# A hash-masked attention block with two gated layers on one core: 1/z of seven head pairs spread over the partitions by a store and two repeating loads in place of transposes

## The chip, the cores and the metric

The kernel runs on one core of a Trainium2 chip. The metric is the device time of one execution in microseconds (us). The core has five engines that run side by side, each through its own queue in order: TensorE (PE, with its weight loads PEld), VectorE (DVE), ScalarE (ACT), GpSimd (POOL) and SyncE (SP), which here only issues DMAs. DMAs issued from SP and from ScalarE's queue share 16 DMA engines.

## What is computed

An attention in which a query sees only the keys of its own hash bucket, then two feed-forward blocks on its output. Shapes: q, k, v are (2, 8, 768, 64), the model width is 512.

```python
q_bits = (np.einsum('bhsd,dk->bhsk', q, proj) > 0).astype(np.int64)
k_bits = (np.einsum('bhsd,dk->bhsk', k, proj) > 0).astype(np.int64)
...
mask = q_bucket[:, :, :, None] == k_bucket[:, :, None, :]
scores = scale * np.matmul(q, k.transpose(0, 1, 3, 2))
scores = np.where(mask, scores, -1000000000.0)
scores = scores - np.max(scores, axis=-1, keepdims=True)
attn = np.exp(scores)
attn = attn / (np.sum(attn, axis=-1, keepdims=True) + 1e-09)
return np.matmul(attn, v).astype(np.float32)
...
gated = u * v_s
return (gated @ w_out).astype(np.float32)
...
ch = np.maximum(xn @ w_ch1, 0.0) @ w_ch2
return (x + ch).astype(np.float32)
```

The change concerns one line of this: the division of the attention by its row sum z.

## The kernel before, in words

Nothing is issued where it is written. Every call goes to a planner (class Plan, lines 170 to 508), which groups calls into jobs, gives each a cost, places them by a list schedule with due times, and then issues them engine by engine in that order (line 502 issues everything, so all rows of the profile have that line). A changed job can therefore move its neighbours on every engine.

The program has three parts. The first holds the attention of both batches, and from its second half on the first feed-forward block of batch 0; the second and third parts hold what is left of the feed-forward blocks. The attention runs over 96 tiles (two batches b, eight heads h, six query tiles of 128); `attn_step(i)` (line 922) writes out one step. For a tile it does: `scores` (line 831), four matmuls of the 128 queries against the 768 keys into the PSUM tile sc; `masked_max` (line 843), which takes sc to SBUF as x and the row maximum nb on VectorE; `exps` (line 862), the exponential on ScalarE, whose row sums go to z_sum; `transposes` (line 868), six TensorE transposes pt of x, copied to e by ScalarE and VectorE. After the six tiles of a head, `weighted` (line 885) multiplies e with v: po, whose result, transposed (features on the partitions, queries along the row), is copied to xT. Two heads form a pair (b, r), and share the 128 partitions of xT[b][:, r]: head 2r has partitions 0 to 63, the other head 64 to 127.

This output still has to be divided by z. z lies with queries on the partitions, xT with queries along the row, so 1/z has to be turned and repeated over 64 partitions. Before the change, `summed` (line 902, one tile behind `weighted`) adds 1e-9 and takes the reciprocal zr, 128 x 12. `normalized` (line 909, three tiles behind) spreads zr on GpSimd to zw, 128 x 384 twice, transposes it on TensorE in six pieces of 128x128 into two PSUM banks pz, and VectorE multiplies xT by each bank. Later `x_split` (line 1052) cuts xT into two parts (act_x) for the feed-forward block.

The loads for the scores go through SP. For a pair, q and k are loaded and split in two parts by GpSimd and VectorE; `passes_of` (line 755) then copies, for each head, the pieces of ks (three of 64x768 and two small ones from the mask tile m, 12 rows) and, for each half of the queries, those of qs. v is loaded as vv. These DMAs stand in one order on SP with the stores of the feed-forward block; a DMA whose source isn't ready holds all behind it. PSUM has four banks with the tag b, shared by pt, po, pm, pz and the first block's results, and two double banks for sc.

The planner costs a DMA of SP by the time to issue it and a landing time by kind (lines 186, 187, 239 to 246), and a transpose like any other of its kind (line 249).

## Time and profile before

| | us |
|---|---|
| median of 3 runs | 646.39 (645.65 to 646.8) |
| the profiled execution | 645.79 |
| its span, first to last instruction | 643.6 |
| TensorE busy | 634.8 (99%) |
| VectorE busy | 500.4 (78%) |
| ScalarE busy | 327.7 (51%) |
| GpSimd busy | 189.6 (29%) |

The granted clock of TensorE is 0.999 over the span. The span leaves out the start and the end of an execution, which is why the time is 2.2 us longer. A share of busy time is a mean over the whole program; the attention stage lies between about 20 and 300 us. In the chain of waits a step is as long as it held up the next one, so its steps can be shorter than an instruction's own record. SP's rows show the time it takes to issue a DMA, not the time of the transfer.

### The profile page before, as it was taken

Reading aid. Unit: us, or ns where it says so; the run is one execution under the profiler, and the core shown is the slowest. Engines: PE = TensorE matmul, PEld = TensorE weight load, DVE = VectorE, ACT = ScalarE, POOL = GpSimd, SP = SyncE. Lnnn points to the kernel's source line nnn. Section 1 sums busy time; section 2 is a strip of 40 time slices with the busy share of each in tenths; the row PEclk is TensorE's granted clock in tenths of the full one; section 3 lists DMA queues with packets and bytes.
Section 4 is the critical chain, followed back from the end, with each engine's and each line's share of the span. In section 5 each row is a group of like instructions: output and inputs, shape, how many; then the busy total and the mean of one; then the engine's idle time right before and its main releaser. Section 6 shows DMA issues by size and latency. Waiting matters only on the chain.

```text
span 643.6 us, 10095 instructions
## 1 busy us (share of the span) xinstructions
PE 634.8 (99%) x3506; PEld 520.3 (81%) x3506; DVE 500.4 (78%) x998; ACT 327.7 (51%) x650; POOL 189.6 (29%) x186
## 2 busy tenths in 40 slices
PE   7999999999999999999999999999999999999997
PEld 5777767777787777877888888899999899898896
DVE  6789878797888686886799544699998887969555
ACT  7888877885565655643555323554323333333110
POOL 2142433244554633131343200122122324142200
PEclk9999999999999999999999999999999999999999
DMA  6776676667767877774653240421262626382623
GB/s 153 195 206 155 181 181 154 183 145 240 204 181 243 235 195 212 228 264 176 231 167 145 73 148 17 147 86 46 99 231 114 234 92 223 105 279 74 218 88 143
DMA packets 64738, 107.68 MB, mean 167 GB/s; under 512 B 7008, under 2 KB 33328, under 8 KB 64432
## 3 DMA queue, kind: packets, MB, share of 16 engines
q1 hardware_dynamic: 43232, 67.58, 36.0%
q10 hardware_dynamic: 21456, 39.46, 18.5%
q8 instruction: 28, 0.46, 0.3%
q14 instruction: 22, 0.18, 0.1%
HBM read 63.31 MB, written 24.90 MB: 137 GB/s over the span
## 4 chain that ended last, share of the span: by engine, by line
PE 94%; DMA 2%; DVE 2%; issue 1%; SPq 0%; POOL 0%; ACTq 0%; DVEq 0%; POOLq 0%
PE acc L502 20%; PE p L502 14%; PE pv L502 10%; PE sc L502 10%; PE pt L502 10%; PE po L502 9%; PE pg L502 7%; PE pc L502 5%; PE py L502 5%; DMA qs<-q 2%; PE pm L502 1%; PE pz L502 1%; PE ptr_g L502 1%; PE px_c L502 1%; DMA pj<-in_proj 1%
## 5 line engine op out<-in xcount | busy, mean ns | idle before, releaser
L502 PE MATMUL acc<-w,ch 128*128 128x512 f32 x576 | 142.9, 393 | 0.0
L502 PEld LDWEIGHTS acc<-w,ch 128*128 128x128 f32 x576 | 107.3, 188 | 18.9
L502 ACT ACTIVATE x<-x,nb 128x768 f32<-128x768 f32 x96 | 89.7, 936 | 31.3 <-DVE x L502 26.4
L502 DVE TENSOR_SCALAR_CACHE_REDUCE x<-sc 128x768 f32<-128x768 f32 x96 | 90.9, 951 | 6.8 <-PE sc L502 3.7
L502 PE MATMUL sc<-ks,qs 128*128 128x512 f32 (+3 forms) x384 | 93.8, 363 | 1.9 <-DVE x L502 1.2
L502 POOL TENSOR_TENSOR f64c_w<-f_w,f64c_w 128x512 f32<-128x512 f32 x32 | 44.1, 1380 | 152.9 <-issue 81.8
L502 PE MATMUL pt<-ident,x 128*128 128x128 f32 x576 | 81.3, 274 | 0.3 <-DVE xT L502 0.3
L502 PEld LDWEIGHTS pt<-ident,x 128*128 128x128 f32 x576 | 66.5, 140 | 14.9 <-issue 2.4
L502 PEld LDWEIGHTS sc<-ks,qs 128*128 128x128 f32 (+1 forms) x384 | 62.9, 190 | 13.9 <-issue 2.2
L502 PE MATMUL po<-e,vv 128*64 128x384 f32 x384 | 65.5, 490 | 0.0
L502 ACT ACTIVATE ch<-u 128x384 fp32r<-128x384 f32 x48 | 25.2, 525 | 79.1 <-DVE u L502 67.0
L502 ACT ACTIVATE e<-pt 128x384 f32<-128x384 f32 x120 | 55.0, 485 | 18.6 <-PE pt L502 18.1
L502 DVE TENSOR_TENSOR u<-p,u 128x384 f32<-128x384 f32 x84 | 45.4, 552 | 20.5 <-PE p L502 20.0
L502 PEld LDWEIGHTS po<-e,vv 128*64 128x64 f32 x384 | 26.1, 137 | 31.2 <-issue 29.8
L502 PE MATMUL p<-t,w 128*128 128x384 f32 x252 | 50.0, 337 | 0.0
L502 PE MATMUL p<-xh,w 128*128 128x384 f32 x252 | 48.8, 338 | 0.0
L502 DVE COPY e<-pt 128x384 f32<-128x384 f32 x72 | 39.7, 553 | 9.6 <-PE pt L502 9.0
L502 PEld LDWEIGHTS p<-t,w 128*128 128x128 f32 x252 | 44.9, 188 | 2.3
L502 PEld LDWEIGHTS p<-xh,w 128*128 128x128 f32 x252 | 44.6, 188 | 2.2 <-DVE u L502 0.3
L502 POOL TENSOR_TENSOR w<-f64c_w,w 128x512 fp32r<-128x512 f32 (+1 forms) x28 | 35.2, 1259 | 37.8 <-ACT w L502 15.0
L502 DVE TENSOR_SCALAR f64c_w<-f64c_w 128x512 f32<-128x512 f32 x64 | 30.8, 480 | 18.5 <-ACT f64c_w L502 15.8
L502 PE MATMUL pg<-vn,w_sp 128*128 128x512 f32 x180 | 43.6, 396 | 0.0
(155 smaller groups left out, 1018.5 us busy)
## 6 DMA issues: line engine op xcount, KB each, us to landing
f_w<-in_w ACTq DMA_DIRECT2D x32, 512.0 KB
ots<-y_dram SPq DMA_DIRECT2D x12, 768.0 KB
ks<-k SPq DMA_DIRECT2D x45, 192.0 KB
y_dram<-ots SPq DMA_DIRECT2D x30, 256.0 KB
qs<-q SPq DMA_DIRECT2D x30, 192.0 KB
wst_sp<-in_w_spT SPq DMA_DIRECT2D x12, 384.0 KB
vv<-in_v SPq DMA_DIRECT2D x16, 192.0 KB
qs<-q SPq DMA_DIRECT2D x30, 96.0 KB
```

The lines of the kernel that those rows point to most:

```text
L502: res = getattr(getattr(nc, engine[j.engine]), op)(*map(live, args), **{k: live(x) for k, x in kw.items()})
```

## The change

`summed` now keeps zr by head, and for seven of the eight pairs does more: one TensorE transpose of the 128 x 12 tile zr into a PSUM bank, a VectorE copy of the 12 x 128 result to zt, a store of zt to a DRAM tile zd, and two loads from zd, each of which repeats one head's row of 768 values over 64 partitions, into zb (128 x 768). `normalized` for such a pair stands eight tiles behind `weighted` in place of three, and is one VectorE multiply of xT by zb, both in SBUF. The last pair (1, 3) keeps the way of before, three tiles behind, with its broadcast in four pieces. There is one buffer each for zt and zb (and the last pair's zw).

```diff
--- before.py
+++ after.py
@@ -901,21 +901,40 @@
 
     def summed(b, r):
 
-        zr = ap.tile([P, NQT, 2], F32, tag="zr", name=f"zr_{b}_{r}")
-        nc.vector.tensor_scalar(zr, z_sum[b][:, :, 2 * r : 2 * r + 2], 1e-9, None, op0=ALU.add)
+        zr = ap.tile([P, 2, NQT], F32, tag="zr", name=f"zr_{b}_{r}")
+        for h in range(2):
+            nc.vector.tensor_scalar(zr[:, h], z_sum[b][:, :, 2 * r + h], 1e-9, None, op0=ALU.add)
         nc.vector.reciprocal(zr, zr)
         pairs[b, r]["zr"] = zr
+        if (b, r) == (B - 1, H // 2 - 1):
+            return
+        rows = 2 * NQT
+        pz = ps_b.tile([P, GW], F32, tag="b", name=f"pz_{b}_{r}")
+        nc.tensor.transpose(pz[:rows, :P], zr.rearrange("p h a -> p (h a)"), ident)
+        zt = ap.tile([rows, P], F32, tag="zt", name=f"zt_{b}_{r}", bufs=1)
+        nc.vector.tensor_copy(zt, pz[:rows, :P])
+        zd = dram.tile([2, 1, S], F32, tag=f"zd_{b}_{r}", name=f"zd_{b}_{r}")
+        nc.sync.dma_start(out=zd.rearrange("h o (a q) -> (h o a) q", a=NQT), in_=zt)
+        zb = ap.tile([P, S], F32, tag="zw", name=f"zb_{b}_{r}", bufs=1)
+        for h in range(2):
+            nc.sync.dma_start(out=zb[h * D : (h + 1) * D], in_=zd[h].to_broadcast([D, S]))
+        pairs[b, r]["zb"] = zb
 
     def normalized(b, r):
 
+        if "zb" in pairs[b, r]:
+            nc.vector.tensor_tensor(xT[b][:, r], pairs[b, r]["zb"], xT[b][:, r], op=ALU.mult)
+            return
         zr = pairs[b, r]["zr"]
+        both = ap.tile([P, S], F32, tag="zw", name=f"zw_{b}_{r}", bufs=1)
         for c in range(2):
-            zw = ap.tile([P, 6, D], F32, tag="zw", name=f"zw_{b}_{r}_{c}", bufs=2)
-            zc = zr[:, c * 3 : c * 3 + 3, :].rearrange("p a (h o) -> p (a h) o", o=1)
-            nc.gpsimd.tensor_scalar(zw, zc.to_broadcast([P, 6, D]), 1.0, 0.0, op0=ALU.mult, op1=ALU.add)
+            zw = both[:, c * KC : (c + 1) * KC].rearrange("p (a h d) -> p a h d", a=3, h=2)
+            for h in range(2):
+                zc = zr[:, h, c * 3 : c * 3 + 3].rearrange("p (a o) -> p a o", o=1)
+                nc.gpsimd.tensor_scalar(zw[:, :, h], zc.to_broadcast([P, 3, D]), 1.0, 0.0, op0=ALU.mult, op1=ALU.add)
             pz = ps_b.tile([P, 3, P], F32, tag="b", name=f"pz_{b}_{r}_{c}")
             for i in range(3):
-                nc.tensor.transpose(pz[:, i, :], zw[:, 2 * i : 2 * i + 2].rearrange("p h d -> p (h d)"), ident)
+                nc.tensor.transpose(pz[:, i, :], zw[:, i].rearrange("p h d -> p (h d)"), ident)
             xs = xT[b][:, r, c * KC : (c + 1) * KC]
             nc.vector.tensor_tensor(xs, pz.rearrange("p a n -> p (a n)"), xs, op=ALU.mult)
 
@@ -934,8 +953,10 @@
             exps(*order[i + 1])
         if 0 <= i - PO < NT and order[i - PO][2:] == (NG - 1, GRP - 1):
             weighted(*order[i - PO][:2])
-        for late, e in ((1, summed), (3, normalized)):
+        for late, e in ((1, summed), (3, normalized), (8, normalized)):
             n = i - PO - late
+            if late > 1 and (late == 8) == (n == NT - 1):
+                continue
             if 0 <= n < NT and order[n][1] % 2 == 1 and order[n][2:] == (NG - 1, GRP - 1):
                 e(order[n][0], order[n][1] // 2)
         n = i + 1 + QA
```

How this moves instructions shows at three places. In the rows, sc is a score tile by head, half and tile, pt the transpose of a tile's exponentials, ks and qs the operands of the scores, pz the transposed 1/z. The first place is TensorE around pair (0, 1), first before, then with the change:

```order
L502 MATMUL pt_4_1_0_0_976<-ident,x_4_1_0_917 128x128 x3
L502 MATMUL pt_4_1_0_1_983<-ident,x_4_1_0_917 128x128 x3
L502 MATMUL sc_4_1_2_992<-ks_4_0_690,qs_4_384_823 128x512 x2
L502 MATMUL sc_4_1_2_992<-ks_4_0_690,qs_4_384_823 128x256 x2
L502 MATMUL pz_1_0_1001<-ident,zw_1_0_947 128x128 x3
L502 MATMUL pz_1_1_1011<-ident,zw_1_1_952 128x128 x3
L502 MATMUL sc_5_0_0_1016<-ks_5_0_857,qs_5_0_912 128x512 x2
L502 MATMUL sc_5_0_0_1016<-ks_5_0_857,qs_5_0_912 128x256 x2
```

```order
L502 MATMUL sc_4_1_2_958<-ks_4_0_675,qs_4_384_807 128x512 x2
L502 MATMUL sc_4_1_2_958<-ks_4_0_675,qs_4_384_807 128x256 x2
L502 MATMUL pt_4_0_2_1_966<-ident,x_4_0_2_883 128x128 x3
L502 MATMUL pz_1_974<-ident,zr_1_853 12x128
L502 MATMUL pt_4_1_0_0_979<-ident,x_4_1_0_907 128x128 x3
L502 MATMUL pt_4_1_0_1_985<-ident,x_4_1_0_907 128x128 x3
L502 MATMUL sc_5_0_0_995<-ks_5_0_843,qs_5_0_902 128x512 x2
L502 MATMUL sc_5_0_0_995<-ks_5_0_843,qs_5_0_902 128x256 x2
```

Two groups of three 128x128 transposes have become one transpose of 12x128, which stands in the run of the pt transposes, earlier in the order.

The second place is SP around pair (0, 3), where the operands of head 2 of batch 1 are copied; before, then with the change:

```order
L502 DMA ks_2_0_1731<-k_1_1_1654 64x768 x2
L502 DMA qs_2_0_1774<-q_1_1_1656 64x2x384
L502 DMA qs_2_0_1774<-m_1_1777 12x384
L502 DMA ks_2_0_1731<-m_1_1777 12x384
L502 DMA ks_2_0_1731<-k_1_1_1654 64x768
L502 DMA qs_2_0_1774<-q_1_1_1656 64x384
L502 DMA ks_2_0_1731<-m_1_1777 12x384
```

```order
L502 DMA ks_2_0_1704<-k_1_1_1640 64x768 x2
L502 DMA zd_3_1725<-zt_3_1707 12x128
L502 DMA qs_2_0_1762<-q_1_1_1636 64x2x384
L502 DMA zb_3_1775<-zd_3_1725 64x768 x2
L502 DMA ks_2_0_1704<-m_1_1760 12x384
L502 DMA qs_2_0_1762<-m_1_1760 12x384
L502 DMA qs_2_0_1762<-q_1_1_1636 64x384
L502 DMA ks_2_0_1704<-k_1_1_1640 64x768
L502 DMA ks_2_0_1704<-m_1_1760 12x384
```

The store of zd and the two loads of zb stand between the first two ks_2 loads and the other DMAs that complete ks_2 and qs_2.

The third place is TensorE where that ks_2 is first read; before, then with the change:

```order
L502 MATMUL sc_1_1_2_1851<-ks_1_0_1547,qs_1_384_1696 128x512 x2
L502 MATMUL sc_1_1_2_1851<-ks_1_0_1547,qs_1_384_1696 128x256 x2
L502 MATMUL pt_1_0_2_1_1857<-ident,x_1_0_2_1788 128x128 x3
L502 MATMUL pt_1_1_0_0_1866<-ident,x_1_1_0_1828 128x128 x3
L502 MATMUL sc_2_0_0_1872<-ks_2_0_1731,qs_2_0_1774 128x512 x2
L502 MATMUL sc_2_0_0_1872<-ks_2_0_1731,qs_2_0_1774 128x256 x2
```

```order
L502 MATMUL sc_1_1_2_1838<-ks_1_0_1535,qs_1_384_1671 128x256 x2
L502 MATMUL pt_1_0_2_1_1844<-ident,x_1_0_2_1770 128x128 x3
L502 MATMUL pt_1_1_0_0_1853<-ident,x_1_1_0_1816 128x128 x3
L502 MATMUL pt_1_1_0_1_1862<-ident,x_1_1_0_1816 128x128 x3
L502 MATMUL sc_2_0_0_1868<-ks_2_0_1704,qs_2_0_1762 128x512 x2
L502 MATMUL sc_2_0_0_1868<-ks_2_0_1704,qs_2_0_1762 128x256 x2
```

The second group of pt_1_1_0 now stands ahead of the first sc_2_0 instead of behind it.

## Rows read from the trace of the kernel before

**Rows 1.** The page's head: span, then busy us (share) x instructions of each engine.
```profile
span 643.6 us, 10095 instructions
PE 634.8 (99%) x3506; PEld 520.3 (81%) x3506; DVE 500.4 (78%) x998; ACT 327.7 (51%) x650; POOL 189.6 (29%) x186
```

**Rows 2.** Waits of TensorE, whole span: us in total, times, longest us.
```profile
PE sc L502 <- DVE x L502: 1.2, 2, 0.9
PE sc L502 <- DMA qs<-q: 0.5, 1, 0.5
PE pt L502 <- DVE xT L502: 0.3, 1, 0.3
```

**Rows 3.** Busy us by stretch, 20 to 300 us; last TensorE clock, DMA share, GB/s.
```profile
20.00:60.00 40.00, 39.48 (x269) 27.96 (x268) 34.41 (x72) 33.16 (x72) 14.06 (x15) 1.00 0.71 181
...
100.00:140.00 40.00, 40.00 (x275) 28.49 (x274) 35.20 (x74) 31.07 (x69) 11.07 (x12) 1.00 0.65 162
...
sum 280.00, PE 278.87 PEld 207.88 DVE 227.17 ACT 188.40 POOL 108.82; mean PE 39.84 PEld 29.70 DVE 32.45 ACT 26.91 POOL 15.55
```

**Rows 4.** Chain of waits, 20 to 60 us: start us, length us, what.
```profile
26.91 5.21 DMA qs<-q
...
46.48 0.24 PE sc L502 x2
46.72 0.66 PE pz L502 x6
47.38 0.70 PE sc L502 x4
48.08 0.33 PE pt L502 x3
```

**Rows 5.** Tiles pz and zr: ns min/median/max, first and last start us, shapes.
```profile
L502 PE MATMUL pz<-ident,zw x48: 269/273/330, 46.6 to 302.6; 128*128 128x128 f32 x48
L502 DVE TENSOR_TENSOR xT<-pz,xT x16: 547/552/558, 47.9 to 303.7; 128x384 f32<-128x384 f32 x16
...
L502 POOL TENSOR_SCALAR zw<-zr x16: 510/512/941, 36.3 to 294.6; 128x384 f32<-128x384 f32 x16
L502 DVE TENSOR_SCALAR zr<-z_sum x8: 161/169/1323, 34.1 to 293.6; 128x12 f32<-128x12 f32 x8
```

**Rows 6.** Groups of VectorE, shapes apart: busy us, mean ns of one; idle before.
```profile
L502 DVE COPY e<-pt 128x384 f32<-128x384 f32 x72 | 39.7, 553 | 9.6 <-PE pt L502 9.0
L502 DVE SCALAR_TENSOR_TENSOR q<-q 128x768 fp32r<-128x768 f32 x7 | 9.2, 1320 | 0.0
...
L502 DVE TENSOR_TENSOR w_sp_early<-wst_sp,w_sp_early 128x768 fp32r<-128x768 f32 x2 | 1.8, 924 | 0.0
```

**Rows 7.** SP in order of time, 128 to 136 us: start us, us to issue.
```profile
128.85 1.12 SPq L502 DMA_DIRECT2D ks<-k  x2
...
132.11 0.80 SPq L502 DMA_DIRECT2D qs<-m  x1
132.96 0.76 SPq L502 DMA_DIRECT2D ks<-m  x1
133.83 0.52 SPq L502 DMA_DIRECT2D ks<-k  x1
134.49 0.51 SPq L502 DMA_DIRECT2D qs<-q  x1
135.06 0.78 SPq L502 DMA_DIRECT2D ks<-m  x1
```

**Rows 8.** Waits of SP for stores to DRAM, whole span: total, times, longest us.
```profile
SPq L502 <- DMA y_dram<-ots: 8.6, 4, 3.7
...
SPq L502 <- DMA y_dram<-ot: 1.6, 1, 1.6
```

**Rows 9.** VectorE and TensorE in order of time, 131 to 140 us.
```profile
131.41 0.67 DVE L502 TENSOR_SCALAR m<-pm,above,worth 128x384 fp32r<-128x384 f32 x1
...
139.61 0.96 PE L502 MATMUL sc<-ks,qs 128*128 128x512 f32 x4
```

## The prediction, made before the changed kernel was run

> **What bounds the kernel now.** I read the page's head first, then the waits of TensorE, then the busy times by stretch, then the chain of waits, and last the timeline around the places that the change touches. The head shows TensorE busy for 634.8 of 643.6 us and the next engine, VectorE, for 500.4 [rows 1]. The list of TensorE's waits is nearly empty: the reader should see three short rows, with nothing above 0.9 us at one time [rows 2]. In the attention stage, 20 to 300 us, TensorE is busy 278.87 of 280 us, VectorE 227.17, GpSimd 108.82, and the DMA engines carry a share of 0.71 in the first stretch [rows 3]. So the rest of the kernel runs into a TensorE queue that is always full, and what leaves that queue in this stage comes off the end. The chain of waits says the same in small: sc, pz and pt follow each other with no step between them, and six pz transposes take 0.66 us of it [rows 4]. The one long DMA step of that chain, 5.21 us for a qs load, is also the one place where TensorE waited for a load, 0.5 us [rows 2, 4].
>
> **The change, part by part.** TensorE loses 42 of the 48 pz transposes (seven pairs of six) and gains seven transposes that write 12x128.
> - Removed: seven times 0.66 us [rows 4] = 4.62 us, all of it on the path.
> - Added: seven times one transpose of zr. No row of before has that form. The nearest is a transpose that streams the same 128 columns inside a run, 0.66 / 6 = 0.11 us [rows 4]; the other end is one that overlaps nothing, its whole record of 273 ns [rows 5]. I take 0.11, since the chain has the queue full on both sides: 0.77 us, with 1.91 as the far end.
> - TensorE together: -4.62 + 0.77 = -3.85 us, or -2.71 at the far end.
>
> The record of one transpose is 273 ns, yet six of them take 0.66 us of the chain, so I price by the chain [rows 4, 5]. The Trainium skill, "TensorE: Matmul & The Clock Gate", section "Part 4: PE-mode transpose", gives about 275 ns for a 128x128 transpose in a kernel's context; taken as the price, the sum would be near -9.6 us, an estimate from that page. The record agrees with the page and the spacing does not.
>
> VectorE loses two multiplies from PSUM of 552 ns per pair, keeps the reciprocal, has two small adds (169 ns) in place of one, and gains a copy of 12x128 (between the 169 ns of a small operation [rows 5] and the 553 ns of a 128x384 copy) and one multiply of 128x768 in SBUF (between 924 and 1320 ns) [rows 5, 6]. Per pair that is +0.16 to +0.92 us, and 1 to 6.4 us over seven pairs, beside 280 - 227 = 53 us in which VectorE is idle in this stage [rows 3]. I cost it at nothing; if that cover were gone, 6.4 us would be the price. GpSimd loses 14 broadcasts of 512 ns [rows 5], 7.2 us; nobody waits for them, so nothing is gained. The last pair keeps its six transposes; its broadcast is cut into four pieces instead of two. In before the last broadcast starts at 294.6 and the last transpose of it at 302.6 us [rows 5], so these eight microseconds hide it and it counts as nothing. The PSUM bank of pz is held for a short copy instead of until a multiply, which can only help.
>
> DMA: each pair adds a store of 6 KB and two loads that repeat a 3 KB row over 64 partitions, 2 x 192 KB. Seven pairs are 2.7 MB; at the 181 GB/s that a share of 0.71 carries [rows 3] the full rate is about 255 GB/s, so this is some 11 us of the 280, and the share goes from about 0.71 to 0.75. Bandwidth has room; landing times may not.
>
> SP is the queue to look at, because it issues in order and a load of zb may not go before the store of zd has landed. In six of the seven pairs, other work or an idle stretch of SP lies between store and load, or nothing behind it is urgent. The tight one is pair (0, 3). In the order of the change, its store stands behind two ks_2 loads, with one qs_2 load after it and then both zb loads, ahead of the five DMAs that complete ks_2 and qs_2. In before, the two ks loads end issuing at 128.85 + 1.12 = 129.97 us, and the last ks<-m ends at 135.06 + 0.78 = 135.84 [rows 7]. A small DMA takes 0.8 us to issue and a ks load 0.56, so with the change the store leaves SP at 130.8, and the zb loads leave 1.1 us after it has landed. How long a landing takes has no row of its own: the shortest wait of SP for a store is 1.6 us, the longest 3.7 [rows 8], and the longest DMA step of the chain 5.2 [rows 4]. At 1.6 us SP is free at 133.5; the five DMAs behind take 3.7 us with their gaps, so the last ends at 137.2, 1.4 us later than before. The mask rows m, for which the first of them waits, are ready at 131.41 + 0.67 [rows 9] and no longer decide. TensorE wants ks_2 at 139.61 [rows 9], 3.8 us after 135.84, and the change puts one more group of three transposes (0.33) ahead of it, so 4.1 us. What is left over is 1.4 plus the landing of that last piece minus 4.1: nothing at a landing of 1.6, 1.1 us at 3.8, which is the most it can have been in before, since TensorE did not wait there. I take 0.4.
>
> The multiplies are the other new wait. Where zb lands late, VectorE stands still and the row maxima behind the multiply come late to ScalarE and so to the pt transposes. The place of the multiply is 14 rows of order behind the zt copy in pair (0, 3) and ten behind the next pair's in pair (0, 0). With 40 us for 74 instructions in that stretch [rows 3], and a second instruction behind each row maximum, these are about 10 and 7 us, against two landings and 2 us of issuing, or one landing and 2 us. At 1.6 us a landing nothing waits, at 3.7 pair (0, 3) is about level. I take 0.2 us in all.
>
> Sum: -3.85 + 0.4 + 0.2 = -3.25 us. The profiled execution took 645.79 us, so 642.5. The median of the runs, 646.39, lies 0.6 above it, which gives 643.1 for a median after. The later stages keep their order nearly unchanged and I let them shift as a block.
>
> **The rivals.**
> - *Part of the gain goes into late landings (0.20).* With a store that lands after 3.7 us, SP comes 3.5 us later to the end of ks_2, and TensorE waits 1.0 to 3.2 us at 139 us, say 2.1. Then -3.85 + 2.1 = -1.75: 644.0 for the profiled run, 644.6 as a median, up to 645.7. For it speaks the share of 0.71 and the chain's qs step; against it that SP's waits in before for stores are few.
> - *TensorE was not what paced the stage (0.09).* Its weight loads are busy only 28.49 us of 40 in the third stretch, and VectorE 35.20 [rows 3]. If matmuls were being held by operands while they count as busy, leaving some out would only lengthen other holds. That would give 646.4. The Trainium skill, "Perfetto Trace Analysis", section "Identifying the Most-Contended Engine", says just this, that matmul busy time is a poor measure and weight-load busy time a better one; by it TensorE would have a quarter to spare here. Against it stand the gapless chain and the empty list of waits [rows 2, 4].
> - *Slower: the store and load hold SP and starve ks_2 (0.10).* One mechanism: if both the store of zd and the last piece of ks_2 take a time L to land, the wait at 139 us is (L - 0.2) + L - 4.1. It eats the whole 3.85 us from L = 4.1 on. At L = 5.2, the longest step of the chain, it is 6.1 us: 645.79 - 3.85 + 6.1 = 648.0, a median of 648.6. For it speaks that the zb loads, 384 KB, stand directly ahead of these pieces; against it, that the 5.2 us occurred once.
> - *Each transpose costs its record (0.01).* (42 - 7) x 0.273 = 9.6 us [rows 5], so 636.8. The chain speaks against it. The figure of the Trainium skill, "TensorE: Matmul & The Clock Gate", section "Part 4: PE-mode transpose", would lead to nearly the same time.
>
> **How the numbers follow.** The forecast has the remaining 0.60: 643.1, by itself 641.7 to 644.0, which is the price ends of the transpose (-2.71 to -3.85) with 0 to 0.6 us of waits, and the spread of the runs of before, 0.7 us down. The range runs from 641.6 to 646.6: it takes in the first two rivals and leaves out the slower case, the transposes at full record and some of each tail, less than 2 in 10. A difference of 0.2%, 1.3 us, is about what a measurement of this kernel can tell from no change. Below 645.1 lie the forecast, most of the late-landing case (0.12) and the last rival: 0.73. Between lie the rest of the late-landing case and most of the second rival: 0.16. Above 647.7: 0.11.
>
> **What would show it.** In the profile after: pz with seven transposes of 12x128 and six of 128x128, TensorE's busy time lower by about 4 us, and its list of waits still short. The rows on which the forecast would fall: a wait of PE sc for a DMA on ks near 136 us, SP waiting for zd by more than 4 us, VectorE xT waiting for zb by more than a microsecond in several pairs, or a TensorE busy time that stays at 634 with fewer instructions, which is the second rival.

## The result and the profile after: slower by 4 us

The changed kernel took 649.86 us (median of 5, 648.74 to 650.07), the kernel before beside it 645.81 (644.83 to 646.8). The ratio is 1.0056 with an interval of 1.0042 to 1.007, so it is slower, by about 3.6 to 4 us. The forecast was 643.1 with a range up to 646.6: wrong in sign. The slower rival had a chance of 0.10 and gave 648.6, but by a mechanism that did not occur, as the runs below show.

First the page's head of the kernel after (span; then busy us, share and instructions of each engine), which answers to [rows 1]:

```profile
span 648.0 us, 10076 instructions
...
PE 634.9 (98%) x3471; PEld 517.3 (80%) x3471; DVE 507.6 (78%) x1006; ACT 327.1 (50%) x650; POOL 186.0 (29%) x174
```

TensorE has 35 instructions fewer and is busy for 634.9 us, against 634.8 before. The prediction had named this row as the one that would show its second rival: a busy time that stays when work is taken away. That fits matmuls which are held by something else and count as busy; the row alone doesn't show it, because the span grew as well.

The parts themselves are as priced. Here are the tiles pz, zt and xT after (durations in ns as min/median/max, then the first and last start in us, and the shapes), which answer to [rows 5, 6]:

```profile
L502 PE MATMUL pz<-ident,zr x7: 272/272/275, 42.7 to 258.9; 128*12 128x128 f32 x7
L502 DVE COPY zt<-pz x7: 268/269/275, 44.6 to 259.9; 12x128 f32<-12x128 f32 x7
...
L502 DVE TENSOR_TENSOR xT<-zb,xT x7: 940/958/1080, 80.0 to 282.1; 128x768 f32<-128x768 f32 x7
```

The copy took 269 ns and the large multiply 958, inside the bounds that were given. TensorE's waits (total, times, longest, in us), against [rows 2]:

```profile
PE sc L502 <- DVE x L502: 1.8, 3, 0.7
PE sc L502 <- DVE f64c_u L502: 1.8, 1, 1.8
PE pv L502 <- DVE e L502: 1.5, 1, 1.5
...
PE p L502 <- DVE u L502: 1.4, 2, 0.8
```

No row names ks, and between 125 and 150 us, around the place that I had picked, its list of waits is empty. And the chain of waits looks different. Its shares between 26 and 136 us, the first half of the attention (batch 0), in the kernel before:

```profile
by line: PE sc L502 32.4%; PE pt L502 29.1%; PE po L502 27.5%; DMA qs<-q 4.7%; PE pm L502 2.8%; PE pz L502 2.4%; SPq L502 0.7%; issue 0.5%
```

and in the kernel after, same view and stretch:

```profile
by line: PE sc L502 22.4%; PE po L502 21.0%; PE pt L502 20.0%; DVE x L502 10.5%; ACT x L502 6.0%; ACT e L502 2.7%; issue 2.4%; DVE f64c_v L502 2.2%; PE pm L502 2.1%; DVE e L502 1.8%; POOL f64c_v L502 1.6%; DVE xT L502 1.6%; DVE q L502 0.9%;
```

Before, the chain is TensorE plus one qs load. After, a tenth of it is VectorE's row maximum x, and 6% ScalarE's exponential. These shares are a hint and no more: e1 and e14 below have the change's order in this stretch and no DMAs of the change, and x has 2.3% of the chain in one and 5.4% in the other. The time can be located better by the starts of the po groups, one for each of the 16 heads, which are the same work in every kernel (from the instructions of tile po in the traces; one profiled execution each, us; "last po" is the start of the last group):

| kernel | first po | first po of batch 1 | last po | first half | second half | last po to the end of the span |
|---|---|---|---|---|---|---|
| before | 25.4 | 133.9 | 298.0 | 108.5 | 164.1 | 345.6 |
| after | 24.7 | 136.3 | 300.2 | 111.6 | 163.9 | 347.8 |
| e9, 42 transposes out | 26.2 | 135.8 | 297.8 | 109.6 | 162.0 | 345.7 |
| e12, 14 multiplies out | 26.3 | 133.9 | 298.5 | 107.6 | 164.6 | 345.7 |
| e13, both out | 26.0 | 133.1 | 295.0 | 107.1 | 161.9 | 346.9 |
| e14, no DMAs, later parts as before | 25.5 | 133.4 | 296.0 | 107.9 | 162.6 | 345.9 |
| e15, e16, e17, first half as before | 26.8, 26.3, 26.5 | 134.7, 134.0, 134.1 | | 107.9, 107.7, 107.7 | | |

The change lost 3.1 us in the first half, gained 0.2 in the second instead of the 1.65 that three pairs should bring, and lost 2.2 after the attention. The last row shows how far one execution can be trusted: e15 to e17 have the first half of the kernel before, and it took 0.6 to 0.8 us less there than in the profile of before. So a tenth or two means nothing here, and the loss in the first half is 3 to 4 us.

### The profile page after: what moved, and what is told of

The parts are those of the page before. It is cut to its first block, busy times and chain, and to the rows that moved or that the text cites. A ratio compares the mean times of both kernels' runs of the same rounds, so it can differ in the third digit from the quotient of the medians.

```text
span 648.0 us, 10076 instructions
## 1 busy us (share of the span) xinstructions
PE 634.9 (98%) x3471; PEld 517.3 (80%) x3471; DVE 507.6 (78%) x1006; ACT 327.1 (50%) x650; POOL 186.0 (29%) x174
## 4 chain that ended last, share of the span: by engine, by line
PE 78%; DVE 8%; DMA 4%; ACT 3%; issue 3%; SPq 1%; POOL 1%; ACTq 0%; DVEq 0%; POOLq 0%
PE acc L502 18%; PE p L502 12%; PE pv L502 9%; PE sc L502 8%; PE po L502 7%; PE pt L502 7%; PE pg L502 6%; PE pc L502 5%; PE py L502 4%; DVE x L502 2%; DMA zb<-zd 2%; ACT x L502 2%; DMA qs<-m 1%; SPq L502 1%; DVE f64c_w L502 1%
## 5 line engine op out<-in xcount | busy, mean ns | idle before, releaser
L502 PEld LDWEIGHTS acc<-w,ch 128*128 128x128 f32 x576 | 107.1, 188 | 19.0
L502 PEld LDWEIGHTS pt<-ident,x 128*128 128x128 f32 x576 | 67.1, 142 | 14.3 <-issue 3.2
L502 PEld LDWEIGHTS po<-e,vv 128*64 128x64 f32 x384 | 26.2, 137 | 31.4 <-issue 29.6
L502 POOL TENSOR_TENSOR w<-f64c_w,w 128x512 fp32r<-128x512 f32 (+1 forms) x28 | 36.6, 1309 | 33.3 <-ACT w L502 13.5
L502 DVE TENSOR_SCALAR f64c_w<-f64c_w 128x512 f32<-128x512 f32 x64 | 36.7, 574 | 11.6 <-ACT f64c_w L502 10.2
```

The costliest lines, as they stand in the source:

```text
L502: res = getattr(getattr(nc, engine[j.engine]), op)(*map(live, args), **{k: live(x) for k, x in kw.items()})
```

## Experiments

Each ratio is to the kernel before, run on the same chip beside it, with its 95% interval. Medians of before were 645.7 to 646.1 in all groups of runs. Where I state a difference of two kernels from different groups, it is a difference of their ratios times 646.

### What the DMAs cost, and by what

**e1: the change without its DMAs.** At issue time, the stores and loads are skipped, and the multiply reads xT twice, so that the kernel leaves the 1/z out of seven pairs.

```diff
                 for op, args, kw in j.calls:
+                    if op == "dma_start" and of(kw["out"])[:3] in ("zd_", "zb_"):
+                        continue
+                    if op == "tensor_tensor" and of(args[1]).startswith("zb_"):
+                        args = (args[0], args[2], args[2])
```

> The changed kernel's own order on every engine, but the seven stores of zd and the fourteen loads of zb are not issued, and the seven multiplies read xT twice in place of zb and xT (so the output lacks the division for these pairs). Theory 1, the added DMAs lose the time: the waits of TensorE near 90, 115, 207 and 297 us go, and the time falls by 4 to 7 us, to 643 to 646. Theory 2, the new order of all other instructions loses the time: nothing changes beyond 1 us, 649 to 650. Theory 3, the multiplies hold VectorE: as theory 1 here, and told apart from it by the next kernel.

Measured: 646.83 us, ratio 1.0019 (1.0009 to 1.0029). The DMAs cost about 0.0037 x 646 = 2.4 us here, but without them the change is still not faster.

**e2: the DMAs stay, the multiply does not wait for them.** Only the second of the two edits of e1.

> The same order, with all stores and loads of zd and zb issued, but no multiply waits for them: the seven multiplies read xT twice (the division is missing for these pairs). Theory 1 (the DMAs delay the loads of ks and qs): 649 to 650 as with the change. Theory 3 (VectorE stands still for zb, 5.3 us in four waits): 1 to 4 us less, 646 to 648.5. Theory 2: 649 to 650.

Measured: 648.84 us, ratio 1.0059 (1.004 to 1.0078), the same as the change. So VectorE's wait for zb, which in the trace after is the row below, costs nothing that can be measured; the DMAs do their harm to others.

```profile
DVE xT L502 <- DMA zb<-zd: 5.3, 4, 2.1
```

**e6 and e7: size or order?** In e6 each load of zb brings 2 partitions; in e7 it is whole, but repeats a row of the input, so that it waits for no store. In both the multiply reads xT twice, as in e2.

```diff
+                    if op == "dma_start" and of(kw["out"])[:3] == "zb_":
+                        kw = {"out": kw["out"][:2], "in_": kw["in_"][:2]}                          # e6
+                        kw = {"out": kw["out"], "in_": qT[0, 0, 0:1].to_broadcast([64, 768])}      # e7
```

> The change in its own order, every DMA kept with its waits, but each load of zb brings 2 partitions instead of 64 (6 KB in place of 192 KB); the multiply reads xT twice, so this kernel leaves the 1/z out of seven pairs. Theory A (the bytes of the repeating loads delay the loads of ks, qs and vv): like the kernel without the DMAs, 646.4 to 647.3. Theory B (the store that has to land holds SP, and what stands behind it goes late): like the kernel whose multiply reads xT but which keeps the DMAs, 648.4 to 649.3. In between, both have a part.

> The change in its own order, the stores of zd kept and both loads of zb at full size, but they repeat a row of the input qT, so that they wait for no store; the multiply reads xT twice, so this kernel leaves the 1/z out of seven pairs. Theory A (the bytes): 648.4 to 649.3, as with the DMAs kept whole. Theory B (SP held until the store has landed): 646.4 to 647.3, as without the DMAs.

Measured: e6 646.65 us, ratio 1.001 (1.0002 to 1.0019), as without the DMAs. e7 649.3 us, ratio 1.0048 (1.003 to 1.0066), as with them whole. It is the size of the loads (e6 cuts their bytes and their rows, 64 of 3 KB, together, so these two are not told apart). The wait of SP for the store of zd, on which the sum and the slower rival rested, is not what costs.

How 192 KB can matter is seen at one place. SP between 78 and 92 us in the kernel after (start us, us to issue):

```profile
81.35 0.50 SPq L502 DMA_DIRECT2D zb<-zd  x1
82.31 0.35 SPq L502 DMA_DIRECT2D vv<-in_v  x1
83.91 1.34 SPq L502 DMA_DIRECT2D qs<-q  x2
85.29 0.79 SPq L502 DMA_DIRECT2D qs<-m  x1
```

and TensorE behind it (the bracket is the idle time before):

```profile
88.30 0.48 PE L502 MATMUL sc<-ks,qs 128*128 128x256 f32 x2
90.54 0.71 PE L502 MATMUL sc<-ks,qs 128*128 128x512 f32 x2 [1.77 <-DVE f64c_u L502]
```

This sc is the first reader of the qs loads issued at 83.91 to 86.08. The bracket names a VectorE instruction, but e6, with the same order and 6 KB in place of 192, issued its qs loads at 84.22 and ran through this place without a wait. The semaphore records of the two traces settle it: the three qs loads had landed at 90.03, 90.41 and 90.59 us in the kernel after, and at 88.50 to 88.88 in e6. TensorE's queue was released at 90.41, and this sc began at 90.54. So qs landed late, behind the zb load and the vv load. (The chain shown above follows the same bracket into VectorE's work, so part of VectorE's share of it is this load.) Where the names are plain they say it: TensorE's waits in e7 between 100 and 120 us and in e2 between 88 and 120 have one row each,

```profile
PE sc L510 <- DMA qs<-q: 1.8, 1, 1.8
```

```profile
PE sc L508 <- DMA qs<-q: 1.4, 1, 1.4
```

against two waits of 0.8 us together in e6 from 80 to 120. The wait has a tail. Stretches of four microseconds (the columns are the busy times of PE, PEld, DVE, ACT and POOL, the granted clock, DMA share, GB/s), after:

```profile
82.00:86.00 4.00, 4.00 (x29) 3.50 (x28) 3.37 (x7) 2.25 (x6) 1.74 (x1) 1.00 0.72 230
86.00:90.00 4.00, 2.78 (x20) 2.25 (x18) 4.00 (x13) 4.00 (x11) 0.00 (x0) 1.00 0.97 213
90.00:94.00 4.00, 3.46 (x16) 3.05 (x17) 1.70 (x4) 1.74 (x4) 1.31 (x1) 0.68 0.48 106
94.00:98.00 4.00, 4.00 (x24) 1.93 (x24) 1.30 (x4) 2.99 (x6) 0.12 (x1) 0.89 0.79 248
```

and in e6:

```profile
82.00:86.00 4.00, 4.00 (x28) 3.19 (x24) 3.34 (x8) 1.93 (x5) 1.73 (x1) 1.00 0.54 174
86.00:90.00 4.00, 4.00 (x29) 3.44 (x29) 4.00 (x12) 4.00 (x10) 0.00 (x0) 1.00 0.96 217
90.00:94.00 4.00, 4.00 (x30) 2.45 (x30) 2.18 (x7) 4.00 (x10) 1.30 (x1) 1.00 0.69 148
94.00:98.00 4.00, 4.00 (x30) 2.76 (x27) 3.19 (x7) 1.68 (x4) 2.75 (x3) 1.00 0.71 232
```

After the wait of 1.77 us TensorE was granted a clock of 0.68 and 0.89 for two stretches, where it has 1.00 in e6, and it got through 16 and 24 matmuls instead of 30. The DMA share of 0.71 in the prediction is a mean: here it is 0.97 and 0.96 for four microseconds in the two kernels, and what is already under way at that moment decides.

The starts of po show that such places are the whole of what the DMAs cost in the first half. All these kernels have the change's order of the attention (us):

| kernel | first to fifth po | fifth to sixth | sixth to ninth | ninth to last | TensorE's waits at these places |
|---|---|---|---|---|---|
| e1, no DMAs | 53.4 | 13.2 | 41.5 | 163.1 | 0.7 at 117 |
| e14, no DMAs | 53.5 | 13.0 | 41.4 | 162.6 | 0.6 at 117 |
| e6, short loads | 53.5 | 13.2 | 41.7 | 162.7 | 0.3 at 117 |
| after | 53.4 | 16.5 | 41.6 | 163.9 | 1.8 at 91, 0.7 at 117 |
| e2 | 53.6 | 14.7 | 43.9 | 163.1 | 1.4 at 91, 1.6 at 120 |
| e3 | 53.4 | 13.9 | 44.0 | 164.2 | 0.6 at 90, 1.8 at 115 |
| e7 | 53.4 | 13.4 | 44.4 | 164.9 | 1.8 at 118 |
| e8, loads from GpSimd | 53.8 | 14.3 | 42.1 | 164.8 | 1.1 at 91, 1.5 at 119 |

Seven pairs load zb, but in the first half only two places lose time, both where a qs load is issued soon after a zb load; how the loss is shared between them differs from execution to execution. With each wait of 1.6 to 1.8 us came stretches of 4 us at a granted clock between 0.68 and 0.89 (after, e2 at 120, e3, e7), and the stretch lost 2.4 to 3.3 us against e1; after the waits of 1.1 to 1.5 us of e2 at 91 and of e8 the clock stayed at 1.00 and the loss was about that of the wait or less.

**e8: the DMAs issued by GpSimd** (the later parts as in e3, below).

```diff
+                    who = "gpsimd" if op == "dma_start" and of(kw["out"])[:3] in ("zd_", "zb_") else engine[j.engine]
```

> The change with its later parts in the order of the kernel before (647.9 us when it was run with its DMAs on SP), and the stores of zd and loads of zb issued by GpSimd instead of SP. Theory B (SP's in-order wait): the loads of ks and qs go on time, and the time falls to about 645, under the kernel before. Theory A (bytes on the shared DMA engines): 647 to 649, no better than on SP. Risk in both: GpSimd stands until the store has landed, and what it computes for VectorE goes late.

Measured: 647.97 us, ratio 1.0037 (1.0025 to 1.005), the same as e3 with its DMAs on SP (1.0036). Freeing SP of the wait brings nothing, which agrees with e6 and e7. Here the loads go through a queue of their own and not through SP's, and TensorE still waits for qs loads (1.8 us in two places). So it is not the place in SP's queue by itself that costs, which leaves the 16 DMA engines that the queues share; that GpSimd, standing for the store, took back a gain elsewhere is not ruled out.

### What the new order costs

**e3: the later parts in the order of before.** The kernel's planner first runs over the old form; parts two and three then take their places from that run.

```diff
+    def pin(self):
...
+        for j, k in self.keys():
+            if j.part < 1:
+                continue
...
+            j.start, j.end = self.pins[k][:2]
```

> The change as it is, with the second and third part of the program (everything after the attention) put into the order that these parts have in the kernel before; the first part keeps the changed kernel's order. After 300 us the changed kernel falls back by another 2 to 3 us against before. If that is its later order: 2 to 3 us less, 647 to 648. If it is a consequence of how the attention ended or of the clock: no change, 649 to 650.

Measured: 647.88 us, ratio 1.0036 (1.0023 to 1.0049). The later order alone costs 0.0020 x 646 = 1.3 us (by the medians 2.0), with an interval from about 0.1 to 2.5. The traces put it nearer to 2: from the last po to the end of the span all kernels with the change's later order take 347.7 to 348.8 us (after, e1, e2, e6, e7), and those with the order of before 345.6 to 346.2, apart from e13 (346.9). The chain of waits from 400 to 640 us shows where it lies. Before it is all TensorE, apart from 0.6% of ots_last; after:

```profile
by line: PE acc L502 42.1%; PE p L502 31.4%; PE pc L502 7.9%; issue 2.7%; DMA f64c_w<-kept 2.4%; PE py L502 2.3%; PE pg L502 1.7%; DVE f_w L502 1.6%; DVE ots L502 1.6%; DVE f64c_w L502 1.5%; DVE u L502 1.3%; PE px_c L502 1.1%; DVE ch L502 0
...
482.32 5.76 DMA f64c_w<-kept
```

In e3 it is TensorE's again. The second row is a weight that is read back from DRAM, with VectorE's work around it. I had not looked at these parts of the order at all: the change has no instruction there, but the planner's times moved, and with them much of the order of VectorE and ScalarE behind the attention.

**e14: e3 without the DMAs**, which tells what is left when both costs are gone.

> The change with the later parts in the order of the kernel before (647.9 us with its DMAs), the stores of zd and loads of zb not issued; the multiply reads xT twice, so this kernel leaves the 1/z out of seven pairs. If the bytes (2 to 3 us) and the later order (2 us) add up: 644.5 to 645.5. If they are not independent: 646 or more.

Measured: 644.72 us, ratio 0.9985 (0.9976 to 0.9994). This kernel is faster than before: the work that the change moves, with the new order of the attention, is worth 1.0 us, the DMAs cost (1.0036 - 0.9985) x 646 = 3.3, the later order 1.3, in all 3.6 us slower. These three must add up to 1.0056, since each is a step from one kernel to the next; taken in the other sequence, by e1, the DMAs cost 2.4 and the later order 2.2, which agrees within the intervals. What is left to explain is why 3.85 us were only 1.0.

### Were the transposes on the path?

**e9: before, without the 42 transposes.** No transpose is put in their place, the multiplies read xT twice, and the order is that of before.

```diff
+                    if op == "transpose" and of(args[0]).startswith("pz_") and not of(args[0]).startswith("pz_1_3"):
+                        continue
+                    if op == "tensor_tensor" and of(args[1]).startswith("pz_") and not of(args[1]).startswith("pz_1_3"):
+                        args = (args[0], args[2], args[2])
```

> The kernel before, in its own order, with the 42 pz transposes of the seven pairs left out and nothing put in their place; their multiplies stay where they were and read xT twice, so this kernel leaves the 1/z out of seven pairs. Theory (TensorE's queue paces the attention): 4.6 us less, 641.2, the lost time of TensorE as before. Rival (TensorE is not the pacer, its holds only move): 644 to 646, with TensorE's list of waits or its busy time grown by what was left out.

Measured: 645.35 us, ratio 0.9994 (0.9984 to 1.0003): no difference, where the prediction had 4.62 us. TensorE's busy time is 634.7 with 42 instructions fewer. Its chain from 26 to 136 us, beside that of before shown above:

```profile
by line: PE po L510 29.7%; PE sc L510 24.6%; PE pt L510 24.3%; DMA qs<-q 4.7%; DVE x L510 4.4%; ACT x L510 2.9%; issue 2.1%; PE pm L510 2.1%; DVE xT L510 1.9%; DVE f_u L510 1.0%; DVE e L510 0.9%; ACT e L510 0.7%; ACT f64c_v L510 0.6%; SPq L
```

With the transposes gone, steps of VectorE and ScalarE come up at once. By the table of po starts the second half became 2.1 us shorter (18 transposes by 0.11 are 1.98), and the first half 1.1 us longer although 24 left it. But e9 does not take away the transposes alone: its multiplies, which now read two operands from SBUF, became longer. VectorE between 20 and 300 us, before and in e9 (busy us, mean ns):

```profile
L502 DVE TENSOR_TENSOR xT<-pz,xT 128x384 f32<-128x384 f32 x14 | 7.4, 551 | 0.0
```

```profile
L510 DVE TENSOR_TENSOR xT<-xT 128x384 f32<-128x384 f32 x14 | 11.2, 825 | 0.0
```

Of these 3.8 us, 0.8 lie in the first half, 0.7 of it in one multiply at 73.5 us, and the head in which it stands took 15.3 us against 14.5 to 14.9 in the kernels with the same order there (before, e12, e13, e15 to e17).

**e12 and e13: the multiplies out; and both out.**

```diff
+                    if op == "tensor_tensor" and of(args[1]).startswith("pz_") and not of(args[1]).startswith("pz_1_3"):
+                        continue                                                                   # e12 and e13
+                    if op == "transpose" and of(args[0]).startswith("pz_") and not of(args[0]).startswith("pz_1_3"):
+                        continue                                                                   # e13
```

> The kernel before with the 14 multiplies by 1/z of the seven pairs left out on VectorE (their output is not scaled), the 42 transposes kept. If VectorE's work paces the first half of the attention: 642 to 644 (four pairs of 1.1 us and less). If TensorE paces it, or both are level: within 1 us of the kernel before.

> The kernel before with both the 42 transposes and the 14 multiplies of the seven pairs left out (their output is not scaled). If TensorE and VectorE are level, so that either alone gains little: clearly less than with the transposes or the multiplies left out alone, 641 to 643. If something else paces (ScalarE, the DMAs): 644.5 to 646.

Measured: e12 645.71 us, ratio 0.9998 (0.999 to 1.0007), no difference. e13 643.76, ratio 0.9969 (0.9957 to 0.9981), 2.0 us less. Between e12 and e13 only the 42 transposes differ, so this pair is the cleaner test: the transposes are worth 0.0029 x 646 = 1.9 us (about 0.9 to 2.8) of the 4.62 forecast.

By the starts of po this gain lies in the second half, which took 161.9 us against 164.6 in e12. Two pairs show their price there:

| us | before, e12 (transposes kept) | e9, e13, e17 (left out) |
|---|---|---|
| tenth to eleventh po, pair (1, 0) | 25.1, 25.1 | 24.4, 24.4, 24.4 |
| fourteenth to fifteenth po, pair (1, 2) | 27.8, 27.8 | 27.1, 27.1, 27.1 |

That is 0.7 us per pair, the 0.66 that the chain gave; the place of pair (1, 1) varies more and shows no such step. In the first half 24 transposes are worth about 0.5 us or less: it took 107.1 in e13 against 107.6 in e12, one execution each, and the kernels of the change's order without large loads, with 20 transposes fewer there, took 107.9 to 108.4 (e1, e6, e14), no less than before. What paces the first half stays open. Two loops that are nearly level, TensorE and the way through VectorE's row maximum, ScalarE's exponential and back, would explain e9 and e12; but e13 takes 2.6 us from the one and 4.4 from the other, and half a microsecond is all that comes of it. That e13 took 1.3 us longer behind the attention is not explained either (one profiled execution).

**e17: the change in the second half alone, without its DMAs**, in the order of before.

> The change in the second half alone without its stores and loads; the multiply reads xT twice, so this kernel leaves the 1/z out of three pairs. If TensorE paces the second half: 15 transposes fewer, 1.65 us, so 644.0 to 645.0. If not: 645.5 to 646.5.

Measured: 644.63 us, ratio 0.9982 (0.9971 to 0.9993): 1.2 us less of the 1.65. So in the second half, TensorE does pace. In the change these 1.65 us shrank to 0.2 for two reasons that the po starts show: a wait of 1.5 us near 210 us for e (the row of pv above), which e1 has too and before does not, so it is the new order; and 0.8 us in the last head, which e1, e6 and e14 do not have, so it is the loads.

### The change by hand in the order of before

**e4, e5, e10, e11.** All engines keep the order of before; the change's instructions are put in at chosen places (pz 2 us after the reciprocal, the copy 0.5 us later in e4 and e5 and 5 us later in e10 and e11, the loads 6 or 10 us after pz, the multiply 15 or 19). e5 and e10 are without the DMAs.

```diff
...
+                    (0, "PE", "transpose", f"pz_{nm}", None, 0, pz),
+                    (0, "DVE", "tensor_copy", f"zt_{nm}", None, 0, pz + 0.5),
+                    (0, "SP", "dma_start", f"zd_{nm}", None, 0, pz + 1.0),
+                    (0, "SP", "dma_start", f"zb_{nm}", None, 0, pz + self.LOADS),
...
```

> The change in the order of the kernel before: every instruction that both have keeps its place of before on each engine, and the new ones are put in by hand (per pair the 12x128 transpose 2 us behind the reciprocal, the store 1 us behind it, both loads of zb 6 us behind the transpose, the multiply 15 us behind it or, for pair (0, 3), just ahead of its first reader). Theory 2 (order): the full gain of 3.9 us less some tenths, 642 to 643. Theory 1 (DMAs): the loads still delay ks and qs, 645 to 649.

> The hand-placed kernel (order of the kernel before everywhere, the change's instructions put in by hand), with the stores of zd and the loads of zb not issued; the multiply reads xT twice, so this kernel leaves the 1/z out of seven pairs. Theory (42 - 7 transposes are worth 3.9 us on TensorE's path, and the DMAs and the new orders take them back): about 3.9 us under the kernel before, 641 to 643, TensorE busy about 4 us less than before and its list of waits as short as before's. Rival (TensorE was not the pacer, its holds only move): within 1 us of the kernel before, with TensorE's busy time near 634.

> As the hand-placed kernel without the DMAs (648.1 us), but the copy of zt stands 4.5 us later in VectorE's order, so that VectorE does not stand behind the po group for pz (4.9 us of such waits in that kernel between 20 and 140 us); the multiply reads xT twice, so this kernel leaves the 1/z out of seven pairs. If that hold of VectorE was the loss: 642 to 643.5. If the loss is in the rest (the transposes were no path, or the 128x768 multiply): 646 to 648.

> The change with the order of the kernel before everywhere, the copy of zt 4.5 us later than in the first hand-placed kernel, the DMAs on SP. If the copy's hold was the loss there and the bytes of the loads cost about 2 us: 644 to 645.5, at or a little under the kernel before. If the transposes were no path: 648 to 650.

Measured: e4 649.78 us, ratio 1.0067 (1.0051 to 1.0082); e5 648.07, 1.0036 (1.0024 to 1.0048); e10 649.01, 1.0045 (1.0028 to 1.0061); e11 654.55, 1.0134 (1.0115 to 1.0152). e5 was the first sign that the term of TensorE was wrong: no DMAs, the order of before, 35 transposes fewer, and 2.3 us slower. VectorE's waits in e5 (20 to 140 us) offered a cause of my own making, the copy of zt standing behind a po group for pz:

```profile
DVE zt L571 <- PE pz L571: 4.9, 2, 3.2
```

e10 moved the copy out of that wait and was not faster, which speaks against this cause. It doesn't rule it out: VectorE's waits at zt and xT together were 6.8 us in this stretch of before, 9.5 in e5 and still 8.2 in e10. What makes the hand-placed kernels slower than e9 stays open; they put a second small add, a copy and a longer multiply at new places into an order of VectorE that was laid out without them. The 4.8 us that e11 took more than e4 lie at one place of the second half, which is also that of e15 below: from the twelfth to the thirteenth po it took 31.5 us, against 26.3 in before.

**e15 and e16: the change in the second half alone, with its DMAs**, by hand in the order of before. In e16 the loads of pair (1, 1) stand behind the load of w_spT.

```diff
-    COPY, LOADS, MULT = 2.5, 6.0, 15.0
+    COPY, LOADS, MULT = 2.5, (6.0, 14.0, 6.0), (15.0, 25.0, 15.0)
```

> The change for the pairs (1, 0) to (1, 2) alone, the other five with the transposes, everything in the order of the kernel before. If TensorE paces the second half: 18 - 3 transposes are 1.65 us less, the loads of three pairs give back up to 1, so 644.3 to 645.5, a little under the kernel before. If the loads cost more, or TensorE does not pace there either: 645.8 or more.

> As the kernel with the change in the second half alone (648.7 us), but the two loads of zb of pair (1, 1) are issued behind the load of w_spT and the qs load that stood behind them, and its multiply 10 us later. If the loads' place was the loss: 644.3 to 645.5, under the kernel before. If the loads lose as much at another place: 647 or more.

Measured: e15 648.73 us, ratio 1.0046 (1.0029 to 1.0062). Its chain has the reason (start, length, what):

```profile
202.41 4.28 DMA zd<-zt
...
207.94 0.79 SPq L563
...
209.33 7.61 DMA wst_sp<-in_w_spT
```

and the waits of ScalarE from 196 to 222 us:

```profile
ACT w_sp L563 <- DMA wst_sp<-in_w_spT: 3.8, 1, 3.8
```

384 KB of weights behind 384 KB of zb took 7.61 us; ScalarE stood for them 3.8 us in its order, and the copies and exponentials behind it with it. In the kernel before, this load was issued at 208.1 us and ScalarE began with it at 212.9, so it took at most 4.8 us; here it was issued at 209.3, and ScalarE began at 217.0. With the loads moved behind it, e16 took 647.38 us (645.6 to 648.98), ratio 1.0018 (1.0005 to 1.003): 1.8 us better than e15, still not under the kernel before, with a wait of 1.7 us for ScalarE's xT left in TensorE's list. No version with the repeating loads beat the kernel before.

## Why the prediction was wrong, step by step

- **"What leaves that queue in this stage comes off the end"** is the step that failed first. The rows were read nearly rightly: a gapless chain and almost no waits [rows 2, 4]. (Over the whole span TensorE has two more waits, of 1.4 and 1.3 us, which [rows 2] leaves out; both lie before 20 us.) They show that TensorE ends last at each step, not by how much. A chain of waits names the one that comes last, by however little; e9 took 24 transposes out of the first half and got nothing, and e13 against e12 got 0.5 us. Of the 3.85 us for TensorE, 1.0 came (e14), and by the table it came in the second half (162.6 us against 164.1). The rival "TensorE was not what paced the stage", at 0.09, was right for the first half, and wrong for the second (e9, e13, e17). The signs stood in [rows 3]: VectorE is busy 33 to 35 us of 40 in the first three stretches, with a fixed order and a round trip through ScalarE, and TensorE's weight loads 28 of 40, against 30 to 32 in the later ones. I set them against the chain and let the chain win. The Trainium skill, "Perfetto Trace Analysis", section "Identifying the Most-Contended Engine", says that the busy share of matmuls is a poor measure of how near TensorE is to its limit, and that of weight loads a better one; the runs here agree on the first, since matmuls were busy for 634.7 us with 42 fewer, while weight loads went from 520.3 to 517.0.
- **VectorE "at nothing", with 53 us of idle time as cover.** No run adds this work alone. That e12 took 14 multiplies, 7.4 us, off VectorE and gained nothing speaks for the term; that one multiply 0.7 us longer went with a head longer by 0.4 to 0.8 (e9) speaks against it, in one execution. The upper end of the sum should also be 6.6 us and not 6.4 (0.169 + 0.553 + 1.320 - 1.104 = 0.94 per pair); nothing hangs on it.
- **GpSimd.** It lost 14 broadcasts and its busy time 3.6 us; no run tested it alone.
- **"Bandwidth has room; landing times may not": 0.4 + 0.2 us.** The concern was right and the price, place and mechanism were wrong. The DMAs cost 3.3 us (e14 and e3). I looked for one queue position, SP held by a store ahead of ks_2 of pair (0, 3); nothing happened there, and SP's wait costs nothing (e7, e8). The two places that lost stand behind the loads of pairs (0, 1) and (0, 2), two of the six pairs that I had passed over because nothing urgent stood behind them. What costs is the size of the zb loads where a qs load comes soon behind them (e6), at two places of the first half, and there the longer waits were followed by a lower clock. The share of 0.71 hid these moments.
- **The multiplies' wait, 0.2 us.** The sign that I had named came, three waits of more than a microsecond and 5.3 us in all, yet they cost nothing (e2). The price is near enough.
- **"The later stages keep their order nearly unchanged and I let them shift as a block."** Untrue, and 1.3 us by e3, or about 2 by the traces. The planner re-sorts all parts from the new times.
- **The slower rival, 648.6 us.** Near the measured time for the wrong reason. It needed landings of 5.2 us near 139 us; the loss lies near 90 and 117 us, in the last head of the second half, and behind the attention.

(The forecast's own bounds come out of its terms as 641.8 to 644.3, not 641.7 to 644.0; that matters as little.) The sum as it should have been: 1.0 us gained in work and the attention's new order, 3.3 lost to the loads, 1.3 to the later order (or 1.0, 2.4 and 2.2, by e1).

## What to carry to other kernels

A chain that lies wholly on one engine says who is last, not how far behind the next one is; before pricing work taken off that engine, leave the work out in one kernel if it can be run, put nothing longer in its place, and read the gain stage by stage: here it came in full in one half and hardly at all in the other. A transfer is priced by the transfers that come soon behind it and by who waits for those, not by the mean share of the DMA engines. Where a planner sets the order, a local change moves all parts, and each must be compared with the order before.

## What the runs showed of the hardware

- TensorE's busy time does not measure its work: 3464 instructions in e9 and 3506 before took 634.7 and 634.8 us, and the same 3464 in e13 631.3.
- After an idle time of 1.77 us TensorE, at 1.00 until then, was granted 0.68 and 0.89 in the next two stretches of 4 us, which mixes its levels of 1.2 and 2.4 GHz. The stretch from the fifth po to the sixth was 3.3 us longer than in e1 for this wait, so a late load can be paid for twice. It need not be: after waits of 1.40 us in e2 (at 91 us) and of 1.07 and 1.48 in e8 the clock stayed at 1.00.
- A load of 384 KB took 7.61 us from issue to landing behind 384 KB of repeating loads (e15), and at most 4.8 in the kernel before. The Trainium skill, "DMA: Bandwidth & Descriptors", section "Queues, rings and completion order", says that transfers issued by SP share one ring on each DMA engine, whose descriptors are consumed in order; that the qs loads are late behind large loads (e7) and not behind small ones in the same place (e6) fits this. The harm does not need the same ring, though: with the loads in GpSimd's queue it is as large (e8, 1.0037 against 1.0036).
- A VectorE multiply of 128x384 with one operand in PSUM took 547 to 558 ns every time in before; the same multiply with xT twice in SBUF took 542 to 1676 ns in e9, 825 in the mean. No run shows what made it longer.
